# Block attention and a GELU MLP on one core: the first tile's order of products, and V of the second tile on two queues

## The chip, the core and the metric

The kernel runs on one core of a Trainium2 chip. A core has TensorE (matrix products into PSUM banks), VectorE, ScalarE and GpSimd, and SyncE (SP), which here only issues transfers. Each engine works through its own list in order and waits on semaphores. 16 DMA engines carry the transfers; SP and ScalarE can both issue them. The metric is the time of one execution on the device, in microseconds. Before the change it was 269.75 us, the median of three runs (269.55, 269.75 and 271.49).

## The reference

Two stages. The first is attention within chunks of 64 keys, for 8 batches, 8 heads, 576 positions and a head size of 64:

```python
q_c, k_c, v_c = (a.reshape(8, 8, 9, 64, 64) for a in (q, k, v))
scores = 0.125 * np.matmul(q_c, k_c.transpose(0, 1, 2, 4, 3))
attn = np.exp(scores - scores.max(-1, keepdims=True))
attn = attn / (attn.sum(-1, keepdims=True) + 1e-09)
out = np.matmul(attn, v_c)
```

The second takes those rows as x, 4608 tokens of 512, and computes `h = x @ w_in` (512 to 2048), `g = 0.5 * h * (1 + erf(h / sqrt(2)))`, and `g @ w_out` (2048 to 512). Inputs and output are float32.

## The kernel before

**Tiles.** The tokens go in 9 tiles of 512. Tile t below 8 holds the first 512 positions of batch t; the last tile holds the ninth chunk of all batches. Each tile passes three stages: attention, which leaves x transposed in SBUF (512 features as 4 slices of 128 partitions, 512 columns of tokens, one slice for each pair of heads); mm1, the product with w_in and the GELU, which leaves h in 16 blocks of 128 features; and mm2, the product with w_out, whose rows are stored. All products run in bfloat16.

**Order.** `tc.manual_schedule()` keeps every engine's instructions in the order in which the program's text issues them. While TensorE does mm1 and mm2 of one tile, the attention of the next one is put between the products, by hand: `phase` takes a table from a slot number to the steps that stand ahead of that slot. So a late operand of a step stops everything behind it on the same engine.

**The first tile** has no tile before it, so its attention stands alone (lines 965 to 1015). Per pair of heads g there are transposes of q and k (`T`), scores (`att_S`), and 1/sum: pairs 0 and 1 by `att_sum` on VectorE, pairs 2 and 3 by `att_sum_pe`, which forms the sums on TensorE, takes the reciprocal on VectorE (`i2`, `i3`) and spreads it over the partitions by 16 float32 products (`p2`, `p3`, line 484); ScalarE copies the result from PSUM (line 487). Then `att_av` multiplies by V (line 498, 64 by 64 products), 32 products for each two pairs, and `att_x` multiplies its result by the reciprocals on VectorE (line 506) and writes x. Where TensorE would stand idle, `keep_warm(n)` (line 958) issues n products of a tile of zeros, 512 columns each; there are 24.

**mm1 of the first tile** begins with `mm1_begin` (line 552): three blocks of h, each the sum of four products of 512 columns over the slices ks of x; first the slices 0 and 1 of all three blocks, then 2 and 3. Their PSUM banks come from the pool `ps_mm`, which has three. `mm1_slot` (line 538) then does block after block. w_in arrives in four chunks of four blocks and is cast to bfloat16 block by block on VectorE, GpSimd and ScalarE (line 939); w_out likewise in four chunks (line 947).

**mm2 of the first tile** (line 891) goes block by block of h over all rows, with the second tile's attention in between: transposes at the slots 2, 3, 4, 7, 8 and 9, scores (line 386) at 8 and 10, AV (line 418) at 13 and 14. ScalarE copies the transposed q and k of the first two pairs (line 178).

**Transfers.** SP issues all loads, in the order of the text. Loads go into five stage buffers of 1 MB, two more hold w chunks; a load waits until the casts from its buffer are done. V of the second tile (`load_v_plain`, line 149) is four transfers of 256 KB behind w_out's chunks; GpSimd casts them (`cast_v_plain`, line 156) behind its casts of w_out.

## Time and profile before

| | before |
|---|---|
| median of three runs | 269.75 us |
| the profiled execution | 270.41 us |
| its span | 268.6 us |
| TensorE busy in the span | 259.6 us, 97% |
| VectorE, ScalarE, GpSimd busy | 202.1, 187.1, 77.0 us |
| first product of mm1 | 18.56 us |
| first product of mm2 | 32.6 us |
| granted TensorE clock | 0.996 of full |

The span is the time from the first to the last instruction of the profiled execution; the rest of its time, 1.8 us, lies around it. All positions below are microseconds from the start of the span. A busy share says how long an engine had work in it, not that this work was needed: the products of zeros count as busy too. "The chain that ended last" follows the last instruction back, at each step to what released it or to the instruction ahead of it on its engine, and so shows what set the end. A row of the timeline merges instructions of one form that follow each other; the time in brackets is how long the engine was idle ahead of them, and what ended that.

### The profile page before, as it was taken

The page shows a single profiled execution, that of the slowest core. Times are in us where ns is not written, and L with a number is a line of the kernel's source. Part 1 is how long each engine was busy: PE and PEld are TensorE (multiplying, and loading weights), DVE is VectorE, ACT ScalarE, POOL GpSimd, SP SyncE. Part 2 cuts the span into 40 slices and gives each one's busy share as a digit, 9 for nine tenths or more (in the row PEclk, how much of TensorE's full clock was granted, in tenths as well). Part 3 has the DMA queues.
Part 4 walks back from the last instruction along what each step waited for, and adds up shares of the span by engine and source line. Part 5 has one row for each costly group of instructions (what it writes and reads, how often), then busy time and mean ns, then how long its engine had stood idle before and what let it go on. Part 6 is the DMA issues. An engine that isn't in the chain of part 4 may idle for free.

```text
span 268.6 us, 7554 instructions
## 1 busy us (share of the span) xinstructions
PE 259.6 (97%) x3077; PEld 195.6 (73%) x3092; DVE 202.1 (75%) x372; ACT 187.1 (70%) x364; POOL 77.0 (29%) x130
## 2 busy tenths in 40 slices
PE   7989999999999999999999999999999999999993
PEld 3554454476548654888888888888888888888882
DVE  2565775989997879589569956995699769958961
ACT  3466756797767967897689669957995799239700
POOL 3735667361440061441044103500362030000000
PEclk9999999999999999999999999999999999999998
DMA  7999999997979959999899989988886760430005
GB/s 230 285 377 402 395 388 243 237 286 194 336 205 261 244 123 231 279 237 191 232 232 231 177 216 242 264 152 206 237 193 146 166 192 0 89 138 12 2 2 156
DMA packets 127075, 56.59 MB, mean 211 GB/s; under 512 B 103488, under 2 KB 120896, under 8 KB 127040
## 3 DMA queue, kind: packets, MB, share of 16 engines
q1 hardware_dynamic: 126592, 55.59, 79.4%
q10 hardware_dynamic: 448, 0.52, 0.7%
q8 instruction: 24, 0.39, 0.6%
q14 instruction: 11, 0.09, 0.1%
HBM read 36.70 MB, written 9.44 MB: 172 GB/s over the span
## 4 chain that ended last, share of the span: by engine, by line
PE 92%; ACT 2%; DVE 1%; DMA 1%; issue 1%; POOL 0%; SPq 0%; ACTq 0%; DVEq 0%; POOLq 0%
PE y_ps L746 24%; PE h_Y L677 15%; PE y_ps L866 12%; PE h_Z L677 10%; PE h_X L677 10%; PE h_ps L538 6%; PE y_ps L891 4%; PE y_ps L755 4%; PE s_ps L247 2%; PE h_ps L699 1%; DMA arrival<-in_k_dram 1%; PE tp L170 1%; ACT y_ps L782 1%; PE warm L958 1%; PE rc_ps L484 1%
## 5 line engine op out<-in xcount | busy, mean ns | idle before, releaser
L677 PEld LDWEIGHTS <-w_in_s 128*128 128x128 bf16 x480 | 46.8, 98 | 6.1
L677 PEld LDWEIGHTS <-w_in_sb 128*128 128x128 bf16 x360 | 35.1, 98 | 6.5
L677 PE MATMUL h_X<-x,w_in_sb 128*128 128x256 bf16 x240 | 33.7, 272 | 0.0
L677 PE MATMUL h_Y<-x_t,w_in_s 128*128 128x256 bf16 x240 | 32.7, 272 | 0.0
L866 PE MATMUL y_ps<-w_out_sb,h 128*128 128x512 bf16 x137 | 31.7, 379 | 0.9 <-issue 0.8
L746 PEld LDWEIGHTS <-h_s 128*128 128x128 bf16 x304 | 29.7, 98 | 3.6 <-issue 0.2
L746 PEld LDWEIGHTS <-h 128*128 128x128 bf16 x288 | 27.8, 98 | 3.4
L218 POOL CAST v_nat<-arrival 128x1024 bf16<-128x1024 f32 x14 | 14.8, 1061 | 48.4 <-DMA arrival<-in_v_dram 48.3
L164 POOL CAST q_nat<-arrival 128x512 bf16<-128x512 f32 x33 | 19.4, 627 | 28.2 <-DMA arrival<-in_q_dram 19.1
L164 POOL CAST k_nat<-arrival 128x512 bf16<-128x512 f32 x34 | 21.9, 678 | 14.0 <-DMA arrival<-in_k_dram 10.1
L746 PE MATMUL y_ps<-w_t,h_s 128*128 128x256 bf16 x208 | 24.8, 273 | 0.0
L866 PEld LDWEIGHTS <-h 128*128 128x128 bf16 x144 | 13.3, 98 | 15.0 <-issue 0.2
L746 PE MATMUL y_ps<-w_out_sb,h 128*128 128x256 bf16 x192 | 22.9, 273 | 0.0
L963 ACT ACT_TABLE_LOAD x16 | 20.5, 1283 | 1.0 <-PEq L1199 0.7
L684 ACT ACTIVATE h<-h_Y 128x512 bf16<-128x512 f32 x30 | 17.7, 595 | 2.4 <-PE h_Y L677 1.9
L714 ACT COPY h_Y<-h_X 128x512 f32<-128x512 f32 x30 | 17.0, 582 | 2.8 <-PE h_X L677 2.6
L684 ACT ACTIVATE h<-h_X 128x512 bf16<-128x512 f32 x30 | 17.8, 597 | 1.4 <-PE h_X L677 0.6
L677 PE MATMUL h_Z<-x_t,w_in_s 128*128 128x256 bf16 x120 | 18.0, 273 | 0.0
L677 PE MATMUL h_Y<-x,w_in_s 128*128 128x256 bf16 x120 | 17.7, 273 | 0.0
L677 PE MATMUL h_Z<-x_t,w_in_sb 128*128 128x256 bf16 x120 | 17.4, 272 | 0.0
L725 DVE COPY h_a<-h_Y 128x512 f32<-128x512 f32 x8 | 5.5, 692 | 14.1 <-PE h_Y L677 14.1
L254 ACT ACTIVATE pT<-s_ps 128x512 bf16<-128x512 f32 x28 | 14.5, 601 | 2.3 <-PE s_ps L247 2.3
(148 smaller groups left out, 489.4 us busy)
## 6 DMA issues: line engine op xcount, KB each, us to landing
arrival<-in_q_dram SPq DMA_DIRECT2D x7, 1024.0 KB
arrival<-in_k_dram SPq DMA_DIRECT2D x24, 256.0 KB
out_dram<-y_sb SPq DMA_DIRECT2D x23, 256.0 KB
arrival<-in_v_dram SPq DMA_DIRECT2D x20, 256.0 KB
arrival<-in_moe_w_out_dram SPq DMA_DIRECT2D x4, 1024.0 KB
arrival<-in_v_dram SPq DMA_DIRECT2D x30, 128.0 KB
out_dram<-y_sb SPq DMA_DIRECT2D x5, 512.0 KB
arrival<-in_moe_w_in_dram SPq DMA_DIRECT2D x4, 512.0 KB
```

Source lines behind the costliest of these rows:

```text
L164: copy(st[nm][:, g].rearrange("p j r d -> p r j d"), st[nm + "f"][:, 2 * g:2 * g + 2])
L218: copy(st["v"][:, part[0], part[1], :D], st["vf"][:, part[0], part[1]])
L254: nc.scalar.activation(pT[:].rearrange("p u (c j) -> p u c j", j=J), s_ps[g2][c][:].rearrange("p u (j c) -> p u c j", j=J), Act.Exp, scale ...
L538: nc.tensor.matmul(h_ps[a][:], w_in_sb[:, ks, f * P:(f + 1) * P], st["x"][:, ks, :], start=(ks == 0), stop=(ks == KS - 1))
L677: nc.tensor.matmul(banks[g + name][:, i], lhs[:, kk, i], rhs[:, kk], start=fresh and i == kk == 0, stop=(kk == 1), skip_group_check=True)
L684: nc.scalar.activation(h[:, j:j + 2, m], src[:], Act.Gelu)
L714: AC(banks[g + "Y"][:], banks[g + "X"][:])
L746: nc.tensor.matmul(out[m], lhs[:, f, m * P:(m + 1) * P], rhs[:, f, :], start=fresh and f == 0 and (m == 0 or len(out) == 3), stop=(f == FH ...
L755: nc.tensor.matmul(out[m], lhs[:, f, m * P:(m + 1) * P], rhs[:, f, :], start=False, stop=(f == FH - 1), skip_group_check=True)
L866: nc.tensor.matmul(y_ps[:], st["h"][:, f, ms * P:(ms + 1) * P], w_out_sb[:, f, :], start=(f == 0), stop=(f == FF - 1))
L891: nc.tensor.matmul(tiles[t]["y_ps", ms][:], tiles[t]["h"][:, f, ms * P:(ms + 1) * P], w_out_sb[:, f, :], start=(f == 0), stop=False)
L963: nc.scalar.activation(act_scratch[:], rest[:, 0:1], func)
```

## The change

In the first tile:

- `att_av` of the pairs 0 and 1 is issued whole, ahead of the second spread `p3`, and `att_x` goes pair by pair: eight operations of 256 columns in place of four of 256 and two of 512.
- Two casts of w_in's first chunk (block 0 on GpSimd, block 1 on ScalarE) stand ahead of `p3`; block 3 goes from VectorE to GpSimd.
- `mm1_begin` takes a list of (block, slice). The products (0,0) and (1,0) come right behind `p3`, ahead of AV of the pairs 2 and 3. Behind that AV come the slices 0 and 1 of four blocks, then slices 2 and 3 of the blocks 0 and 1 and of 2 and 3. The fourth block's bank comes from `ps_at`, and each GELU is issued where its block is complete.
- `keep_warm` issues four products of 128 columns for each one of 512, and the tile of zeros is 128 columns wide.

In the second tile:

- Two of V's four transfers, and their casts, move to slot 5 of the first tile's mm2; ScalarE issues them, behind its copies of the slots 2 to 4.
- The casts of w_out's second chunk swap VectorE and GpSimd.

```diff
-    rest = consts.tile([P, 512], bf16, name="rest")
+    rest = consts.tile([P, P], bf16, name="rest")
...
-    def load_v_plain(t):
-        tiles[t]["vf"] = stage_tile()[:].rearrange("p (h n d) -> p h n d", h=H, d=D)
-        for n in range(CT // 2):
-            nc.sync.dma_start(tiles[t]["vf"][:, :, n], v[t, :, P * n:P * (n + 1), :].rearrange("h key d -> key h d"))
+    def load_v_plain(t, ns=range(CT // 2), engine=nc.sync):
+        if 0 in ns:
+            tiles[t]["vf"] = stage_tile()[:].rearrange("p (h n d) -> p h n d", h=H, d=D)
+        for n in ns:
+            engine.dma_start(tiles[t]["vf"][:, :, n], v[t, :, P * n:P * (n + 1), :].rearrange("h key d -> key h d"))
...
-    def att_x(t, g2, c, ns):
+    def att_x(t, g):
         st = tiles[t]
-        def part(p):
-            return p.rearrange("p g (n c e) -> p g n c e", c=2, e=CH)[:, :, ns[0]:ns[-1] + 1, c]
-        nc.vector.tensor_tensor(part(st["x"][:, 2 * g2:2 * g2 + 2]), st["av", g2][c][:, :, ns[0]:ns[-1] + 1],
-                                part(st["rcs", g2][:]), op=mybir.AluOpType.mult)
+        x, rc = (p.rearrange("p (n c e) -> p n c e", c=2, e=CH) for p in (st["x"][:, g], rc_of(t, g)))
+        for c in range(2):
+            nc.vector.tensor_tensor(x[:, :, c], st["av", g // 2][c][:, g % 2], rc[:, :, c], op=mybir.AluOpType.mult)
...
-    def mm1_begin(t, n):
+    def mm1_begin(t, order):
         st = tiles[t]
-        st["h"] = hpool.tile([P, FF, MT], bf16, tag="h", name="h")
-        h_ps = [ps_mm.tile([P, MT], f32, tag="mm", name="h_ps") for _ in range(n)]
-        order = [(f, ks) for k2 in range(2) for f in range(n) for ks in (2 * k2, 2 * k2 + 1)]
+        if "h" not in st:
+            st["h"] = hpool.tile([P, FF, MT], bf16, tag="h", name="h")
+            st["h_ps"] = {}
         for f, ks in order:
-            nc.tensor.matmul(h_ps[f][:], w_in_sb[:, ks, f * P:(f + 1) * P], st["x"][:, ks, :],
+            if ks == 0:
+                pool, tag = (ps_at, "at") if f == 3 else (ps_mm, "mm")
+                st["h_ps"][f] = pool.tile([P, MT], f32, tag=tag, name="h_ps")
+            nc.tensor.matmul(st["h_ps"][f][:], w_in_sb[:, ks, f * P:(f + 1) * P], st["x"][:, ks, :],
                              start=(ks == 0), stop=(ks == KS - 1))
-        for f in range(n):
-            nc.scalar.activation(st["h"][:, f, :], h_ps[f][:], Act.Gelu)
+            if ks == KS - 1:
+                nc.scalar.activation(st["h"][:, f, :], st["h_ps"][f][:], Act.Gelu)
...
-        for _ in range(n):
-            nc.tensor.matmul(warm[:], rest[:, 0:P], rest[:], start=True, stop=True)
+        for i in range(n * MT // P):
+            nc.tensor.matmul(warm[:, i % 4 * P:(i % 4 + 1) * P], rest[:], rest[:], start=True, stop=True)
...
-        att_av(0, 0, (0, 1))
-        for c in range(2):
-            att_x(0, 0, c, (0, 1))
+        att_av(0, 0)
+        att_x(0, 0)
+        att_x(0, 1)
+        win[0](0, PO)
+        win[0](1, AC)
         p3()
-        att_av(0, 0, (2, 3))
-        for c in range(2):
-            att_x(0, 0, c, (2, 3))
-        att_av(0, 1, range(4))
-        for c in range(2):
-            att_x(0, 1, c, range(4))
+        mm1_begin(0, [(0, 0), (1, 0)])
+        att_av(0, 1)
+        att_x(0, 2)
+        att_x(0, 3)
         win.append(load_w_in(NWC - 1))
         wout = [load_w_out(0)]
-        win[0](0, PO)
-        win[0](1, AC)
         act_table(Act.Gelu)
         win[0](2, PO)
-        win[0](3, DV)
-        mm1_begin(0, 3)
+        win[0](3, PO)
+        mm1_begin(0, [(0, 1), (1, 1), (2, 0), (2, 1), (3, 0), (3, 1)]
+                  + [(f, ks) for f2 in (0, 2) for ks in (2, 3) for f in (f2, f2 + 1)])
...
-        load_v_plain(1)
+        load_v_plain(1, (0, 1))
...
-            wout[1](i, DV if i % 2 == 0 else PO)
+            wout[1](i, DV if i % 2 == 1 else PO)
...
-        cast_v_plain(1, PO)
+        cast_v_plain(1, PO, (0, 1))
...
-                      2: [T[0]], 3: [T[2]], 4: [T[4], T[6]], 7: [T[1], T[3]], 8: [T[5], lambda: duo_S(1, 0)],
+                      2: [T[0]], 3: [T[2]], 4: [T[4], T[6]],
+                      5: [lambda: load_v_plain(1, (2, 3), nc.scalar), lambda: cast_v_plain(1, PO, (2, 3))], 7: [T[1], T[3]], 8: [T[5], lambda: duo_S(1, 0)],
...
-              by_rows=True, begun=3)
+              by_rows=True, begun=4)
```

9 lines of the change are left out of this document (4 added, 5 removed).

## The prediction

> **What bounds the kernel now.** I read the page first: TensorE's share, the engine shares of the chain that ended last, and TensorE's waits.
>
> ```profile
> span 268.6 us, 7554 instructions
> ...
> PE 259.6 (97%) x3077; PEld 195.6 (73%) x3092; DVE 202.1 (75%) x372; ACT 187.1 (70%) x364; POOL 77.0 (29%) x130
> ...
> PE 92%; ACT 2%; DVE 1%; DMA 1%; issue 1%; POOL 0%; SPq 0%; ACTq 0%; DVEq 0%; POOLq 0%
> ...
> PE av_ps L498 <- issue: 0.7, 1, 0.7
> ```
>
> TensorE carries 92% of the chain, so the time falls only where TensorE idles or works for nothing. Its longest single wait, after the one for its first operand, is in AV of the first tile (line 498), and it waits there for nothing that the profile shows. The change edits the first 47 us, so I read the chain there in order of time (start, us, what).
>
> ```profile
> 5.87 2.10 PE warm L958 x7
> 7.97 0.22 PE tp L170 x4
> 8.19 0.43 PE warm L958 x2
> ...
> 16.12 1.09 PE rc_ps L484 x16
> 17.22 0.44 PE av_ps L498 x39
> 17.66 0.70 issue
> 18.35 0.29 PE av_ps L498 x9
> ...
> 20.08 1.46 PE h_ps L552 x6
> 21.54 8.42 PE h_ps L538 x39
> ...
> 41.23 0.38 PE s_ps L386 x32
> 41.61 0.32 PE y_ps L891
> ...
> 47.49 0.38 PE av_ps L418 x32
> ```
>
> From 21.54 on the matmuls of 512 columns follow each other at 8.42/39 = 0.216 us and nothing waits: steady state. Before that, between the end of the second reciprocal spread (16.12 + 1.09 = 17.22) and 21.54, TensorE does 48 small AV products and 12 large ones, some 0.6 + 2.6 us of work in 4.3 us. That is where there is something to take.
>
> **The first tile, step by step.** The timeline has what each step needs (start, us, engine, line; idle before).
>
> ```profile
> 15.30 0.61 POOL L939 CAST w_in_sb<-arrival 128x512 bf16<-128x512 f32 x1 [0.73 <-DMA arrival<-in_moe_w_in_dram]
> ...
> 15.69 0.59 ACT L487 COPY rcs<-rc_ps 128x512 f32<-128x512 f32 x1 [0.48 <-PE rc_ps L484]
> ...
> 15.75 0.32 PE L498 MATMUL av_ps<-pT,v_nat 64*64 64x64 bf16 x16
> 15.86 0.21 DVE L477 RECIPROCAL rr<-sT 128x8 f32<-128x8 f32 x1 [0.51 <-PE sT L472]
> ...
> 16.13 0.76 DVE L506 TENSOR_TENSOR x<-av_ps,rcs 128x256 bf16<-128x256 f32 x2
> 16.62 0.61 POOL L939 CAST w_in_sb<-arrival 128x512 bf16<-128x512 f32 x1 [0.71 <-DMA arrival<-in_moe_w_in_dram]
> ...
> 17.27 0.59 ACT L487 COPY rcs<-rc_ps 128x512 f32<-128x512 f32 x1 [0.99 <-PE rc_ps L484]
> ...
> 17.75 0.62 ACT L939 CAST w_in_sb<-arrival 128x512 bf16<-128x512 f32 x1
> ...
> 18.56 2.97 PE L552 MATMUL h_ps<-x,w_in_sb 128*128 128x512 bf16 x11
> ```
>
> All 32 products of AV's first half now stand ahead of the spread. At 0.38/32 = 0.012 us each they end at 15.75 + 0.38 = 16.13; the spread waits for the reciprocal until 16.07 anyway, so it starts at 16.12 as before and ends at 17.22. Then:
>
> - x of head pair 0 is two VectorE operations of 256 columns, 16.13 + 0.76 = 16.89; pair 1 ends at 17.65. w_in's block 0 is cast at 15.91. Block 1 moves ahead of the second rcs copy on ScalarE: 16.28 + 0.62 = 16.90, and the copy behind it still starts at 17.27. Products (0,0) and (1,0) run 17.22 to 17.65.
> - AV's second half: 0.38, to 18.03, if the 0.70 does not come back. Its x follows on VectorE: pair 2 from 18.03 to 18.79, pair 3 to 19.55. Four operations of 256 cost 1.52 where two of 512 cost 1.30; the 0.22 stays under matmuls.
> - Six products on pairs 0 and 1, 6 x 0.216: 18.03 to 19.33. Block 2 is cast at 17.23, block 3, now on GpSimd behind it, at 17.84; the third bank of the pool is free when the rcs copy ends at 17.86. Pair 2 is needed at 19.33 (ready 18.79), pair 3 at 19.76 (ready 19.55, the tightest, 0.2 us to spare).
> - Eight more end at 21.05. All of four blocks are then done. Before, three were done at 21.54 and the fourth at 21.54 + 4 x 0.216 = 22.40.
>
> Gain **1.35 us**: 0.70 the gap, 0.2 AV moved into the wait for the reciprocal, 0.2 the wait for x (six products from 18.56 should end at 19.86; the next starts at 20.08), the rest the six that took 1.46 instead of 1.30.
>
> **The 0.70 gap** is the term without a price of its own, 0 to 0.70. What I see: the instruction queue q8 moves 24 packets in the whole execution (page), one of them between 16.0 and 17.2 us (DMA queues of that stretch); and TensorE has issued 222 + 223 instructions by the gap (stretches from the start).
>
> ```profile
> q8 instruction: 24, 0.39, 0.6%
> ...
> q8 instruction: 1, 0.02, 4.6%
> ...
> 8.78 0.32 PE L433 MATMUL s_ps<-qT,kT 64*64 64x64 bf16 x16
> ...
> 0.00:12.10 12.10, 10.16 (x96) 4.97 (x97) 4.75 (x10) 4.36 (x9) 6.29 (x21) 1.00 0.89 252
> 0.00:17.60 17.60, 15.46 (x222) 8.76 (x223) 8.30 (x19) 7.18 (x16) 8.70 (x24) 1.00 0.94 282
> ```
>
> A starved instruction stream fits: (3077 + 3092)/24 = 257 instructions a packet, so q8 feeds TensorE, and the gap comes where small products use instructions fastest. If a packet is asked for some 250 instructions ahead of its use, this one was asked for near instruction 193, at 12.1 us, and could be used at 18.35: 6.2 us. The 24 fillers of two instructions become 96, 144 instructions more. By the changed order, instruction 193 is then the end of the first scores (8.78 to 9.1 in this trace), and 445 is the start of AV's first half at 15.7. 9.1 + 6.2 = 15.3 is in time by 0.4 us. I take the gap as gone, nearer to this count than to "it stays"; the other end is 0.70. [...]
>
> **Fillers.** Their number is fixed, so columns count. Four transposes of 128 columns take 0.22 us and two fillers of 512 take 0.43, so a filler costs 0.22 instead of 0.215; nine on the chain lose 0.05 us. The shorter memset lets the first begin sooner, under the load of the first k, which ends later.
>
> **Carrying it on.** TensorE arriving 1.35 us earlier must find its inputs. The rows that set the tightest ones (a stretch with its DMA share and GB/s last, then the timeline):
>
> ```profile
> 31.00:42.00 11.00, 10.89 (x102) 5.93 (x102) 8.16 (x15) 6.82 (x12) 8.50 (x13) 1.00 1.03 352
> ...
> 25.55 1.62 POOL L939 CAST w_in_sb<-arrival 128x512 bf16<-128x512 f32 x2 [0.95 <-DMA arrival<-in_moe_w_in_dram]
> ...
> 31.41 10.61 SPq L149 DMA_DIRECT2D arrival<-in_v_dram  x4
> ...
> 33.40 1.55 POOL L947 CAST w_out_sb<-arrival 128x512 bf16<-128x512 f32 x2 [0.28 <-DMA arrival<-in_moe_w_out_dram]
> ...
> 36.92 1.07 ACT L178 COPY qT<-tp 128x512 bf16<-128x512 bf16 x2 [0.50 <-PE tp L170]
> ...
> 38.69 3.73 POOL L947 CAST w_out_sb<-arrival 128x512 bf16<-128x512 f32 x6 [0.97 <-DMA arrival<-in_moe_w_out_dram]
> ...
> 39.96 1.07 ACT L178 COPY kT<-tp 128x512 bf16<-128x512 bf16 x2 [1.96 <-PE tp L170]
> ...
> 45.70 0.63 POOL L156 CAST v_nat<-arrival 128x512 bf16<-128x512 f32 x1 [0.94 <-DMA arrival<-in_v_dram]
> ...
> 261.20 3.96 ACTq L847 DMA_DIRECT2D out_dram<-y_sb  x4
> ```
>
> The last w_in chunk is cast by 27.2; its first block is needed at 21.05 + 8 x 0.866 = 27.98. The second w_out chunk lands at 33.40, and the swap of VectorE and GpSimd has its first block cast at 34.2, needed near 35.8. The third is cast from 38.69, its first block by 39.31; it was needed at 41.61, now at 40.26: 0.95 to spare. V's last quarter is cast at 46.33; AV was at 47.49, now 46.14: 0.19 short if V stayed where it was.
>
> **V's second half** goes behind the qT copies on ScalarE's queue: 37.99 - 1.35 = 36.64. Queued behind it are the kT copies, which S waits for (41.03 to 41.23, 0.2 spare). ScalarE has 1.96 us free there, and the four issues at the kernel's end took at most 3.96/4 = 0.99 each, so two fit, just. SP's own four took 10.61/4 = 2.65 each in this stretch; that is the upper end, 5.3 us, and I take the lower because the row is ScalarE's own. For that the data passes the third and fourth w_out chunks: 0.52 MB at the 352 GB/s of this stretch moves them by up to 1.5 us. If the flow starts one issue later, at 37.6, the third chunk still had 1.1 us to run; at half rate that is 2.2, and its first block is cast at 40.41 against 40.26: **0.15 lost**, bounds 0 and 0.55 (38.69 + 1.5 + 0.62 = 40.8). V's casts follow the w_out casts: 38.69 + 3.73 + 4 x 0.65 = 45.0, at worst 46.5, 0.2 past AV's 46.14 + 0.15; I take none.
>
> SP, two issues shorter, goes on to q and k of the third tile sooner. GpSimd casts them after V, and nothing of them stands in the chain shown. If their bytes fill the engines while V's second half flows, that half shares with them instead of with w_out; its casts have 46.14 - 45.0 = 1.1 us for it.
>
> **Sum.** -1.35 + 0.05 + 0.15 = **-1.15 us**. The span becomes 267.45; the profiled execution, 270.41 for a span of 268.6, becomes 269.26. That execution lies 0.66 above the median of the three runs, 269.75, so the median becomes **268.6** (-0.4%). Nothing behind 50 us changes but its start.
>
> **Rivals.**
> - *The gap stays* (it belongs to AV's stream, or the earlier fetch is late all the same): -0.45, 269.3. For it: it sits in the second AV half, which still follows an uneven stretch. Against: the 144 instructions.
> - *ScalarE's queue blocks*, the slower side: each issue takes SP's 2.65 because the engines are full. The kT copies come 5.3 - 1.96 = 3.3 us late, S 3.1, and the 0.15 hides in it: 268.45 + 3.1 = 271.6. It decides from 1.1 us an issue; past 1% it needs some 3.1 us each. A single issue of 4.90 stands on SP's queue; two such would give 276. For it: the DMA share of 1.03 in that stretch. Against: SP's issues take long behind a backlog on SP's own queue; ScalarE's queue holds nothing before these two.
>
> ```profile
> 19.83 4.90 SPq L944 DMA_DIRECT2D arrival<-in_moe_w_out_dram  x1
> ```
>
> - *The change does not reach the chain*: the early products wait for x or bank and only reorder; the x of pair 3 late by 0.5. With 0.4 of the gain gone: 269.0. Against: the slacks above, of which only that 0.2 is thin.
>
> **How the numbers follow.** Forecast (268.1 to 268.9) 0.6; the gap stays or the reorder gives less 0.22; ScalarE blocks 0.12, a third of it past 1%; better than 268.0, 0.06. A measurement of this kernel tells about 1%, 2.7 us, from nothing. The sum never reaches that, so faster 0.03, same 0.92, slower 0.05. The range takes in the gap's return and the small end of blocking: 267.9 to 270.2. ScalarE blocking in full, 271.6 and up, lies above it, and the 0.06 below 268.0 is half outside.
>
> **What will show it.** Right: TensorE's wait list without line 498 or its like near 15.7; the fourth block's last product near 21.1; first w_out product near 31.4 instead of 32.76; S near 39.9. Wrong: a gap of 0.3 us or more before 22 us; DMA issues over 1 us on ScalarE near 37 us with S behind them; the third w_out chunk's cast after 40.3; a fetch gap at another dense stretch.

## The result and the profile after

The changed kernel takes **271.6 us** in the median (270.21 to 273.75), against 270.08 for the kernel before on the same chip (269.35 to 272.52). The ratio is 1.005, with a 95% interval of 1.0028 to 1.0073: by the ratio some 1.35 us slower, where 1.15 us faster was forecast, and outside the forecast range of 267.9 to 270.2. It is within 1%, as the chances said, but of the other sign, and the interval excludes no change.

The page of the changed kernel: its span, the busy time of TensorE, two DMA queues (packets, MB, share of the engines) and the chain's shares by engine.

```profile
span 270.1 us, 7702 instructions
...
PE 259.6 (96%) x3150; PEld 199.7 (74%) x3164; DVE 203.8 (75%) x373; ACT 187.2 (69%) x364; POOL 79.7 (30%) x131
...
q10 hardware_dynamic: 2528, 1.05, 1.5%
q8 instruction: 25, 0.41, 0.6%
...
PE 83%; DMA 7%; SPq 4%; issue 1%; POOL 1%; ACT 1%; DVE 0%; ACTq 0%; POOLq 0%
```

TensorE's busy time is what it was, 259.6 us. Its share of the chain fell from 92% to 83%, and DMA's rose from 1% to 7%: TensorE now waits for data. Its list of waits says where (total, times, longest).

```profile
PE av_ps L419 <- POOL v_nat L157: 0.7, 2, 0.3
...
PE h_ps L554 <- POOL w_in_sb L941: 0.3, 1, 0.3
PE h_Z L679 <- DVE h_d L730: 0.3, 1, 0.3
```

The wait of 0.70 in AV for "issue" is gone. Three others are new: for w_in's cast, for V's casts in the second tile, and for a VectorE operation on `h_d`, far behind the part that was edited. TensorE's timeline in the first tile shows the forecast order.

```profile
15.47 1.09 PE L485 MATMUL rc_ps<-ident_f,rr 128*64 128x128 f32 x16
16.84 0.60 PE L554 MATMUL h_ps<-x,w_in_sb 128*128 128x512 bf16 x2 [0.28 <-POOL w_in_sb L941]
17.37 0.45 PE L498 MATMUL av_ps<-pT,v_nat 64*64 64x64 bf16 x32
17.75 3.37 PE L554 MATMUL h_ps<-x,w_in_sb 128*128 128x512 bf16 x13
20.97 0.81 PE L537 MATMUL h_ps<-x,w_in_sb 128*128 128x512 bf16 x3
```

Four blocks are done at 21.13, forecast 21.05. The first w_out product starts at 31.33, 1.27 us ahead of the kernel before (32.60), forecast 1.35. That the places agree is luck. This execution had its first scores at 8.12 and its second spread at 15.47, where the kernel before, and with it the forecast, had 8.78 and 16.12. From the first scores to the first w_out product it is 23.21 us against 23.82: the reorder and the lost gap of 0.70 together brought 0.61; the other 0.66 of the lead is the earlier start. What the forecast had beyond that was waited away at w_in, as GpSimd's timeline shows:

```profile
16.17 0.61 POOL L941 CAST w_in_sb<-arrival 128x512 bf16<-128x512 f32 x1 [1.92 <-DMA arrival<-in_moe_w_in_dram]
17.57 1.17 POOL L941 CAST w_in_sb<-arrival 128x512 bf16<-128x512 f32 x2 [0.79 <-DMA arrival<-in_moe_w_in_dram]
```

Block 0 is cast at 16.78 and block 3 at 18.74, forecast 15.91 and 17.84. The lead of 1.27 stands until AV of the second tile begins at 46.15 (before: 47.42). It is spent as follows (start of the same step in both traces).

| step | before | after | lead |
|---|---|---|---|
| AV of the second tile, first half | 47.42 | 46.15 | 1.27 |
| AV of the second tile, second half | 48.76 | 48.67 | 0.10 |
| mm1 of the third tile | 54.51 | 54.24 | 0.27 |
| first w_out product behind the `h_d` wait | 120.78 | 120.87 | -0.09 |
| last product | 263.67 | 263.72 | -0.05 |
| end of span | 268.59 | 270.11 | -1.52 |

So there are three places: 1.17 us at V, 0.36 at `h_d`, 1.47 behind the last product. The chain in order of time shows the first (start, us, what).

```profile
32.06 11.94 DMA arrival<-in_v_dram
...
44.66 0.93 issue
...
45.61 1.76 POOL v_nat L157 x3
...
47.41 0.35 PE av_ps L419 x20
```

GpSimd's timeline of the same stretch, first of the kernel before, then of the changed one:

```profile
42.37 1.31 POOL L156 CAST v_nat<-arrival 128x512 bf16<-128x512 f32 x2
43.98 0.79 POOL L156 CAST v_nat<-arrival 128x512 bf16<-128x512 f32 x1 [0.30 <-DMA arrival<-in_v_dram]
```

```profile
44.05 0.61 POOL L157 CAST v_nat<-arrival 128x512 bf16<-128x512 f32 x1 [0.22 <-DMA arrival<-in_v_dram]
45.61 1.75 POOL L157 CAST v_nat<-arrival 128x512 bf16<-128x512 f32 x3 [0.95 <-DMA arrival<-in_v_dram]
```

Before, V's quarters land one behind the other (42.09, 43.00, 43.92 and 45.65 by the transfers' semaphores). Three are cast by 44.77, and one cast stands behind the last landing (it starts at 45.70, as the prediction's lines show): V is ready at 46.33. After, the second half is issued on ScalarE's queue at 36.01, but its first packet flows at 39.70, 0.39 us behind the first packet of the first half (39.31), and from there the two halves flow beside each other. Quarters 2, 0, 3 and 1 land in this order, at 43.51, 43.99, 45.29 and 45.55. The last landing is where it was before. But GpSimd casts in the order 0, 1, 2, 3, so it waits 0.95 us for quarter 1 while 2, and then 3, lie ready, and three casts stand in a row behind it: 47.36.

The second place, by VectorE's timeline of before and of after:

```profile
118.36 0.69 DVE L725 COPY h_d<-h_Y 128x512 f32<-128x512 f32 x1 [0.16 <-PE h_Y L677]
119.17 0.69 DVE L728 TENSOR_TENSOR h_d<-h_Z,h_d 128x512 f32<-128x512 f32 x1
```

```profile
118.09 0.69 DVE L727 COPY h_d<-h_Y 128x512 f32<-128x512 f32 x1 [0.16 <-PE h_Y L679]
119.25 0.69 DVE L730 TENSOR_TENSOR h_d<-h_Z,h_d 128x512 f32<-128x512 f32 x1 [0.47 <-PE h_Y L679]
```

From the copy's start to the addition's it is 0.80 before and 1.16 after. In the trace of after the semaphore wait ahead of the addition is over at 118.84, and the addition starts at 119.25: nothing that the profile names fills the 0.4 us.

The third place, by the DMA queues between 266.0 and 268.5 (packets, MB, share):

```profile
q10 hardware_dynamic: 173, 0.14, 17.3%
q1 hardware_dynamic: 105, 0.08, 10.9%
q8 instruction: 1, 0.02, 2.2%
```

TensorE's 25th instruction packet (16 KB) flows from 266.23 to 267.11, among the last stores. All store packets end by 266.92 except the last 20. These start at 267.10, where the instruction packet ends, and end between 267.24 and 268.19, strictly one behind the other. That they stood behind it on one DMA engine is argued from this order and not shown: the trace doesn't name the engine. Before, with 24 packets, the last store landed 3.1 us behind the last product; here it is 4.5.

### The profile page after: what moved, and what is told of

Read it like the earlier page. It is cut to its first block, busy times and chain, and to the rows that moved or that the text cites. A ratio compares the mean times of both kernels' runs of the same rounds, so it can differ in the third digit from the quotient of the medians.

```text
span 270.1 us, 7702 instructions
## 1 busy us (share of the span) xinstructions
PE 259.6 (96%) x3150; PEld 199.7 (74%) x3164; DVE 203.8 (75%) x373; ACT 187.2 (69%) x364; POOL 79.7 (30%) x131
## 4 chain that ended last, share of the span: by engine, by line
PE 83%; DMA 7%; SPq 4%; issue 1%; POOL 1%; ACT 1%; DVE 0%; ACTq 0%; POOLq 0%
PE y_ps L748 24%; PE h_Y L679 15%; PE y_ps L868 11%; PE h_Z L679 10%; PE h_X L679 10%; PE h_ps L537 5%; DMA arrival<-in_v_dram 4%; PE y_ps L757 4%; DMA arrival<-in_moe_w_in_dram 2%; SPq L150 2%; PE s_ps L248 2%; SPq L108 1%; PE h_ps L701 1%; ACT y_ps L784 1%; PE h_ps L554 1%
## 5 line engine op out<-in xcount | busy, mean ns | idle before, releaser
L219 POOL CAST v_nat<-arrival 128x1024 bf16<-128x1024 f32 x14 | 16.8, 1202 | 47.5 <-DMA arrival<-in_v_dram 47.4
```

Source lines behind the costliest of these rows:

```text
L219: copy(st["v"][:, part[0], part[1], :D], st["vf"][:, part[0], part[1]])
```

## The experiments

Theories at the start: **E**, the packet at the end makes the loss; **V**, moving V's half makes it; **I**, which came up later, the `h_d` wait belongs to VectorE's instruction count; **D**, the first 50 us go at the pace of the data, so that a lead is waited away. The expectations name further ones with their rivals. Ratios are to the kernel before on the same chip, with their 95% interval. An interval is some 0.5% wide (1.3 us), so a step of 0.4 us has to be read from a trace. The kernel before against itself gave 1.001.

| kernel | median us | ratio | first w_out product | V ready, AV starts |
|---|---|---|---|---|
| before | 270.08 | | 32.60 | 46.33, 47.42 |
| `before_again` | 270.83 | 1.0010 (0.9985 to 1.0035) | 32.03 | 47.04, 46.85 |
| after | 271.60 | 1.0050 (1.0028 to 1.0073) | 31.33 | 47.36, 46.15 |
| `after_again` | 271.32 | 1.0031 (1.0007 to 1.0055) | 32.91 | 49.86, 48.70 |
| `fewer` | 271.59 | 1.0052 (1.0026 to 1.0078) | 32.23 | 48.53, 47.08 |
| `more` | 271.88 | 1.0056 (1.0033 to 1.0079) | 32.06 | 48.83, 46.88 |
| `v_split_only` | 270.68 | 1.0020 (1.0005 to 1.0036) | 31.82 | 48.76, 47.02 |
| `fillers_only` | 270.95 | 1.0023 (1.0000 to 1.0046) | 32.04 | 47.55, 47.05 |
| `v_on_sp` | 270.78 | 1.0011 (0.9985 to 1.0036) | 32.18 | 47.90, 47.34 |
| `reorder_only` | 270.78 | 1.0009 (0.9990 to 1.0029) | 31.94 | 46.36, 46.75 |
| `chunk_out` | 270.60 | 1.0001 (0.9978 to 1.0024) | 31.70 | 45.32, 46.52 |
| `casts_swapped` | 270.92 | 1.0021 (0.9997 to 1.0045) | 32.61 | 48.02, 47.75 |
| `after_dve` | 270.87 | 1.0014 (0.9994 to 1.0035) | 32.91 | 48.43, 47.73 |
| `before_less_dve` | 270.59 | 1.0011 (0.9985 to 1.0038) | 32.62 | 46.93, 47.44 |
| `reorder_cast_dve` | 271.15 | 1.0027 (1.0001 to 1.0053) | 33.25 | 46.94, 48.07 |
| `reorder_dve` | 269.86 | 0.9978 (0.9955 to 1.0000) | 31.49 | 46.72, 46.31 |
| `v_on_sp_dve` | 270.76 | 0.9999 (0.9971 to 1.0027) | 31.89 | 47.64, 47.06 |
| `q2_behind` | 279.70 | 1.0342 (1.0310 to 1.0375) | 32.63 | 50.55, 48.73 |
| `reorder_spare` | 277.89 | 1.0288 (1.0246 to 1.0330) | 32.83 | 49.61, 48.33 |
| `v_on_sp_spare` | 278.77 | 1.0306 (1.0265 to 1.0347) | 31.90 | 50.12, 48.93 |

### The packet at the end

`fewer` takes instructions off TensorE, `more` adds some; the columns stay.

```diff
-    def keep_warm(n):
+    def keep_warm(n, cols=P):
         warm = ps_mm.tile([P, MT], f32, tag="mm", name="warm")
-        for i in range(n * MT // P):
-            nc.tensor.matmul(warm[:, i % 4 * P:(i % 4 + 1) * P], rest[:], rest[:], start=True, stop=True)
+        for i in range(n * MT // cols):
+            k = i * cols % MT
+            moving = rest[:, 0:cols] if cols <= P else rest[:, 0:1].to_broadcast([P, cols])
+            nc.tensor.matmul(warm[:, k:k + cols], rest[:, 0:P], moving, start=True, stop=True)
...
-        keep_warm(7)
+        keep_warm(7, MT)
         T = att_units(0, DV, AC)
```

> The changed kernel, with the first 28 fillers of 128 columns replaced by seven of 512: 42 instructions fewer on TensorE, the same columns. Theory E (a 25th instruction packet of 16 KB, fetched at 266.24 us, stands ahead of the last stores' packets on one DMA engine and lands them 1.4 us late): 24 packets, the last near 256, the last store packet ends some 1.4 us sooner against the last matmul, time 271.6 - 1.4 = 270.2. Rival N (the late landing is chance, or belongs to something else in the change): 271.6, and the end as late as in the changed kernel.

```diff
-        keep_warm(7)
+        keep_warm(7, 64)
         T = att_units(0, DV, AC)
```

> The changed kernel, with the first 28 fillers of 128 columns replaced by 56 of 64: 56 instructions more on TensorE, the same columns. Theory E: still 25 packets, but the last is asked for 56 instructions (28 products of 512 columns at 0.216 us, 6.0 us) sooner, near 260.2, when no store waits for its engine; the last store packet ends as in the kernel before, 270.2 in all. Rival M (each further packet costs, wherever it falls, or longer streams cost): 271.6 or more. Rival N (chance): 271.6.

The traces did what E says: 24 packets in `fewer`; in `more` the 25th at 260.49 (forecast 260.2); in both the last store lands 3.1 us behind the last product. The times did not follow: 271.59 and 271.88. So the late end belongs to that one execution. The same happened once more, in `v_on_sp_dve` (packet at 266.14, 4.5 us); with the same TensorE stream the packet came behind the stores in `v_on_sp` (270.70), and not at all in `after_again`.

> The changed kernel again, for a second profile. By what the variants showed: first w_out product between 31.3 and 32.2, V's last cast between 47.4 and 48.8, AV's wait 0.7 to 1.3, 0.3 for h_d near 119. The late end (theory E: a 25th instruction packet among the last stores, 1.4 us): if it is what makes the median, it is there again and the last store lands 4.5 us behind the last product; if it falls where it falls from execution to execution, 3.1 us.

There the last store lands 3.1 us behind the last product. The first product of w_out, at 32.91, and V, at 49.86, came later than I had expected. **E explains the 1.47 us in that trace and nothing of the median**, though the two agree to 0.1.

### V's half, and its casts

> The changed kernel, with the second half of V back on SP behind the first and its casts with the first half's: one part undone. Theory V (the half on ScalarE's queue makes three quarters of V land together, so that three casts stand in a row ahead of AV): V's last cast ends near 46.3 as in the kernel before, AV waits 0.2 instead of 1.2, and 1.0 us more of the lead is left at 50 us: 271.6 - 1.0 = 270.6, with the late end (theory E) still in it. Rival B (the bytes ahead of V are the same on either queue and the engines are full, so that V's last quarter lands at 45.6 whichever queue has it and AV waits the same): 271.4 to 271.6.

```diff
-        load_v_plain(1, (0, 1))
+        load_v_plain(1)
...
-        cast_v_plain(1, PO, (0, 1))
+        cast_v_plain(1, PO)
...
-                      5: [lambda: load_v_plain(1, (2, 3), nc.scalar), lambda: cast_v_plain(1, PO, (2, 3))], 7: [T[1], T[3]],
+                      7: [T[1], T[3]],
```

270.78 in place of 271.6, a ratio of 1.0011 in place of 1.0050, and AV waits 0.3 where the changed kernel, `after_again`, `fewer` and `more` wait 0.7 to 1.3. V counts. The 1.0 that should be left at 50 us is not there, though: this trace is 0.27 behind the kernel before at mm1 of the third tile, since it had waited 0.8 for w_in and 0.3 for w_out on the way. It loses another 0.55 at 74.96, by a wait for "issue" that comes up again under the first tile.

> The kernel before with the second half of V on ScalarE's queue and nothing else of the change. Theory V (the half moved makes V land late and in a lump): AV of the second tile waits 0.3 to 1.0 for V's casts, time 270.55 + 0.3 to 1.0 = 270.9 to 271.5. Rival (V on that queue is harmful only with the lead of the reorder in front of it): 270.5, AV's wait unchanged.

```diff
-        load_v_plain(1)
+        load_v_plain(1, (0, 1))
...
+                      5: [lambda: load_v_plain(1, (2, 3), nc.scalar), lambda: cast_v_plain(1, PO, (2, 3))],
```

Even without the reorder in front of it the half is harmful: AV waits 1.1, as theory V says. The time is less clear: 270.68 lies between what the theory and its rival forecast, and the ratio of 1.0020 is small, though its interval excludes 1. GpSimd's timeline and TensorE's waits of `v_split_only`:

```profile
45.44 0.62 POOL L157 CAST v_nat<-arrival 128x512 bf16<-128x512 f32 x1
47.00 1.76 POOL L157 CAST v_nat<-arrival 128x512 bf16<-128x512 f32 x3 [0.95 <-DMA arrival<-in_v_dram]
```

```profile
PE av_ps L419 <- POOL v_nat L157: 1.1, 3, 0.4
```

The same picture as in the changed kernel: one cast, 0.95 of waiting, three casts in a row. Two theories of it were tried against each other.

> The changed kernel with GpSimd's casts of the second tile's V in the order 0, 2, 3, 1 instead of 0, 1, 2, 3. In the changed kernel's profile the quarters 2 and 3 had landed on ScalarE's queue by 44.95 while GpSimd waited for quarter 1 until 45.61, and three casts then stood in a row to 47.36. Theory L (the lump: quarter 1 lands last, and two casts that could have gone before it go behind it): the last cast ends one cast behind the last landing, 1.1 us sooner against it; AV waits 0.1 to 0.3 instead of 0.7 to 1.3, 271.6 becomes 270.5. Rival Q (all four quarters land late, since q of the third tile flows beside them; the order matters little): 271.3 or more, AV's wait at least 0.6.

```diff
-        cast_v_plain(1, PO, (0, 1))
+        cast_v_plain(1, PO, (0,))
...
-                      5: [lambda: load_v_plain(1, (2, 3), nc.scalar), lambda: cast_v_plain(1, PO, (2, 3))], 7: [T[1], T[3]],
+                      5: [lambda: load_v_plain(1, (2, 3), nc.scalar), lambda: cast_v_plain(1, PO, (2, 3, 1))], 7: [T[1], T[3]],
```

```profile
45.71 2.31 POOL L157 CAST v_nat<-arrival 128x512 bf16<-128x512 f32 x4 [0.25 <-DMA arrival<-in_v_dram]
```

In GpSimd's timeline of `casts_swapped` the pause of 0.95 is gone, the four casts follow each other, V is ready 0.27 behind AV's start (1.21 in the changed kernel), and AV is not on TensorE's list of waits of 0.2 us or more. This trace runs later than the changed kernel's, so the two can't be compared by their times; but in it the quarters land at 45.66, 47.11, 44.93 and 46.73. In the old order the three casts behind quarter 1 would have ended near 47.11 + 1.8 = 48.9 (an estimate from the changed kernel, whose three casts end 1.8 behind that landing), 0.9 later than they did. 270.92, where L said 270.5; the interval of 0.9997 to 1.0045 touches that of the changed kernel, so the trace carries this more than the time does.

> The changed kernel with SP held, ahead of its loads of the third tile's q and k, until V's last cast (a copy of one row of it into a spare tile stands in front of them). Theory Q (with two issues less on SP, q of the third tile starts 3 us sooner and takes its share of the engines from V): V's last quarter lands 0.8 us or more sooner, AV waits 0.3 or less; 271.6 becomes 270.5, unless the third tile's own casts, 5 us later, are then waited for. Theory L: V lands as late as in the changed kernel, since the four quarters share the engines among themselves, and the three casts in a row stay: AV waits 0.7 or more, 271.3 or more.

```diff
+        hold = consts.tile([1, D], bf16, name="hold")
         def next_qk():
+            nc.sync.dma_start(hold[:], tiles[1]["v"][0:1, 0, 3, :D])
             for nm in "qk":
                 load_qk(2, nm)
```

With no byte of the third tile beside it V landed no sooner (48.8), and the row of three casts stayed. That speaks against Q, but weakly: this kernel ran with slower transfers for another reason (a 2 KB packet took 88.8 ns where the changed kernel's took 84.2; below), and its 279.7 says nothing on V. How much the third tile's q takes from V stays open.

> The changed kernel with the load of the fourth w_out chunk (1 MB) left out; its casts read the third chunk's arrival, so the output's second product is not the reference's. Theory D: V's bytes come 2.6 us sooner, AV of the second tile waits for no cast, 1.2 to 1.9 us are kept at 50 us and 271.6 becomes 269.7 to 270.4. Rival (V is late by its casts' order on GpSimd or by ScalarE's issue, not by the bytes ahead): the wait of 0.7 to 1.3 in AV stays, 271.2 or more.

```diff
-    def load_w_out(c):
-        raw = stage_tile(wsum if c > 1 else None)[:].rearrange("p (f n) -> p f n", f=FC)
-        nc.sync.dma_start(raw, w_out_v[:, c * FC:(c + 1) * FC, :])
+    def load_w_out(c, held={}):
+        if c == 2:
+            held["raw"] = stage_tile(wsum)[:].rearrange("p (f n) -> p f n", f=FC)
+        raw = held["raw"] if c > 1 else stage_tile()[:].rearrange("p (f n) -> p f n", f=FC)
+        if c != 3:
+            nc.sync.dma_start(raw, w_out_v[:, c * FC:(c + 1) * FC, :])
```

This kernel leaves out the load of one w_out chunk and serves for its time alone. With 1 MB less ahead of it V is ready at 45.32, AV waits for nothing, and 0.9 is kept to 120 us. 270.60, ratio 1.0001: by the ratio about 1.3 us off the changed kernel, as D said, but some 0.36 of it is the `h_d` wait, which this kernel does not have either. It then lost 1.3 us of its own at later places (0.27 near 140, 0.5 near 205, 0.55 near 220), which were not followed up.

### The first tile

> The kernel before, unchanged, for a second profile. The profiles of the changed kernel and of its four variants so far all had 5.2 to 5.6 MB moved by 20 us, that of the kernel before 5.9, and w_in, w_out and V follow that flow. Theory S (the early instruction packet at 10 us, which the 144 further instructions bring, takes its engine from the first loads): again 5.8 to 5.9 MB by 20 us and V's last cast near 46.3. Rival (the early flow varies by itself): anything from 5.2 to 5.9, and V's last cast up to 1.5 us later.

The early flow varies by itself: this trace moved 5.46 MB by 20 us and had V ready at 47.04, where the first trace of the same kernel had 5.93 and 46.33. Theory S is not excluded by that: seven traces with fillers of 512 columns moved 5.3 to 5.9 MB by 20 us, ten with smaller ones moved 5.1 to 5.7 (`fewer` and `more` among the ten, the three kernels with an added tile left out). The stretch from 0 to 20 us, last columns TensorE's clock, DMA share and GB/s, in the kernel before, in `before_again` and in `after_again`:

```profile
0.00:20.00 20.00, 17.12 (x236) 9.53 (x239) 10.23 (x23) 9.43 (x19) 9.31 (x25) 1.00 0.95 296
```

```profile
0.00:20.00 20.00, 17.65 (x239) 9.84 (x242) 10.81 (x24) 9.44 (x19) 9.04 (x25) 1.00 0.93 273
```

```profile
0.00:20.00 20.00, 18.08 (x314) 13.77 (x315) 10.09 (x24) 9.53 (x19) 9.26 (x25) 1.00 0.85 253
```

The trace that the prediction was made from had the fastest early flow of all. It also had a gap of 0.70 in AV that not every execution of this kernel has. TensorE's timeline of `before_again`:

```profile
16.01 1.09 PE L484 MATMUL rc_ps<-ident_f,rr 128*64 128x128 f32 x16
17.04 0.77 PE L498 MATMUL av_ps<-pT,v_nat 64*64 64x64 bf16 x48
18.22 2.75 PE L552 MATMUL h_ps<-x,w_in_sb 128*128 128x512 bf16 x11 [0.41 <-DVE x L506]
```

AV's 48 products run with hardly a break; TensorE then waits 0.41 for x, and the first w_out product stands at 32.03, 0.57 sooner than in the first trace. In the four traces with AV's order and the fillers of before, the instruction packet flows from 16.04 to 16.92 (gap 0.7), from 14.75 to 16.25 (`before_again`), from 13.90 to 15.32 (`v_split_only`, none) and from 16.18 to 17.14 (`before_less_dve` below, gap 0.9). Where TensorE stops it stops ahead of the same product, the 56th of AV's 64, and goes on 1.2 to 1.4 us behind the end of the packet: at 18.35, at 18.37, and in `before_again`, where only 0.18 us is lost, at 17.53. One more stop of this kind stands in `v_on_sp`, behind the AV of a later tile, 1.3 us behind a packet that ends at 73.66:

```profile
74.96 3.41 PE L868 MATMUL y_ps<-w_out_sb,h 128*128 128x512 bf16 x15 [0.55 <-issue]
```

So in these traces the gap goes with a late instruction packet, as the prediction took it; what was wrong is to take its size for a property of the kernel.

> The changed kernel with fillers of 512 columns again and V whole on SP: the reorder alone. Theory D (the first 50 us go at the pace at which w_in, w_out and V land, so that a lead on TensorE is mostly waited away): first tile up to 0.65 sooner (the gap of 0.70 is back somewhere, since the instruction count is that of the kernel before), at 50 us at most 0.4 ahead, and 270.1 to 270.7 against 270.55 for the kernel before. With S the early flow is that of the kernel before (5.8 to 5.9 MB by 20 us) and it is the fastest so far. Rival P (TensorE's own work sets the pace, the terms of the prediction hold): 0.65 kept to the end, 269.9 or less.

```diff
-    rest = consts.tile([P, P], bf16, name="rest")
+    rest = consts.tile([P, 512], bf16, name="rest")
...
-        for i in range(n * MT // P):
-            nc.tensor.matmul(warm[:, i % 4 * P:(i % 4 + 1) * P], rest[:], rest[:], start=True, stop=True)
+        for _ in range(n):
+            nc.tensor.matmul(warm[:], rest[:, 0:P], rest[:], start=True, stop=True)
```

(and V on SP, as above.) 270.78, ratio 1.0009. TensorE's waits of `reorder_only`:

```profile
PE h_ps L554 <- POOL w_in_sb L941: 0.8, 1, 0.8
...
PE h_Z L679 <- DVE h_d L730: 0.3, 1, 0.3
```

The early products stand where they should, and wait for w_in's blocks. At the first w_out product this trace is 0.66 ahead of the first trace of before, which has the gap, and 0.09 ahead of `before_again`, which hardly has it; 0.35 goes at `h_d`. The median of 270.78 is neither D's 270.1 to 270.7 nor P's 269.9, but nearer to D. From the first scores to the first w_out product it took 23.4 us in the traces with the old order and no gap (`before_again`, `v_split_only`, `fillers_only`). With the new order it took 22.7 to 24.7, on average of eleven traces 23.6 (`reorder_cast_dve` and the three kernels with an added tile left out). The 22.7 stand in `reorder_dve` and `after_dve`, the only two in which TensorE has no wait of 0.2 us or more for w_in. So the order by itself can save 0.7 us, and mostly doesn't, because the landing of w_in ends last: D is borne out in the first tile.

> The kernel before with the fillers of 128 columns and nothing else of the change: 144 instructions more on TensorE. Theory E: 25 packets, the last at the end of TensorE's stream in the middle of the last stores, which land 1.4 us late. Theory F (the gap of 0.70 in AV of the first tile is a fetch, whose place goes with the number of instructions): no gap in AV's second half. With both: start 0.2 to 0.66 sooner by the fillers, gap 0.70 gone, V at most 0.2 late, end 1.4 late: 270.1 - 0.9 to 1.3 + 1.4 = 270.2 to 270.6. Without E: 268.8 to 269.2. Without F: 0.7 more in either case.

```diff
-    rest = consts.tile([P, 512], bf16, name="rest")
+    rest = consts.tile([P, P], bf16, name="rest")
...
-        for _ in range(n):
-            nc.tensor.matmul(warm[:], rest[:, 0:P], rest[:], start=True, stop=True)
+        for i in range(n * MT // P):
+            nc.tensor.matmul(warm[:, i % 4 * P:(i % 4 + 1) * P], rest[:], rest[:], start=True, stop=True)
```

No gap, as F says; but 24 packets and not the 25 of E, and 270.95 is outside both forecasts (270.2 to 270.6, 268.8 to 269.2). With a ratio of 1.0023, its interval from 1.0000, and 1.0011 against 1.0009 for the reorder with and without them, the fillers' own effect is not settled; by the interval it is under 0.5%.

### VectorE's instruction count

> The reorder alone (fillers of 512, V on SP) with one more small memset on VectorE at the start, so that its instruction count is that of the kernel before. Theory I (the addition into h_d that starts 0.4 us behind its semaphore near 119 us is the place at which VectorE's instruction stream crosses a block; one instruction less ahead of it, the cast of w_in's block 3 that went to GpSimd, put the crossing there): TensorE's wait for h_d near 119 us is gone; 0.35 us better than the reorder alone, 270.4 against 270.78. Rival (the wait belongs to the arrival time of something else): the wait of 0.3 near 119 us stays.

```diff
     nc.vector.memset(rest[:], 0.0)
+    nc.vector.memset(rest[:, 0:2], 0.0)
```

**269.86**, ratio 0.9978. TensorE's waits of `reorder_dve` are, behind the first operand, these two, and the lead of 0.91 at mm1 of the third tile is 1.01 at the last product:

```profile
PE av_ps L420 <- POOL v_nat L158: 0.2, 1, 0.2
PE sum_ps L446 <- ACT pT L439: 0.2, 1, 0.2
```

> The kernel before with one instruction less on VectorE: the cast of w_in's block 3 in the first tile on GpSimd. Theory I (whatever instruction is number 192 of VectorE's stream starts some 0.4 us late; with one less it is the addition into h_d for which TensorE waits, with the full count it is the semaphore wait in front of it, where the time is hidden): a wait of 0.3 for h_d near 119 us appears in a kernel whose order is otherwise that of before, and the median goes up by 0.35 to 0.85 us, ratio 1.0013 to 1.003. Rival (the wait belongs to the reorder): no such wait, ratio 1.000.

```diff
         win[0](2, PO)
-        win[0](3, DV)
+        win[0](3, PO)
```

```profile
PE av_ps L498 <- issue: 0.9, 1, 0.9
PE h_Z L677 <- DVE h_d L728: 0.3, 1, 0.3
```

TensorE's waits of `before_less_dve`, above: the wait for `h_d` appears in a kernel that is otherwise the one before. The time between the starts of the `h_d` copy and the addition is 1.14 to 1.16 in every trace with one instruction less on VectorE (after, `after_again`, `fewer`, `more`, `v_on_sp`, `reorder_only`, `casts_swapped`, `q2_behind`, `before_less_dve`) and 0.79 to 0.80 in every one with the old count. `chunk_out`, with two less, also has 0.80. In the stream, number 192 is the addition with one less, behind a short semaphore wait. With the old count it is that semaphore wait, behind the copy of 0.69 us; with two less it is the next addition, behind one of 0.69 us. That the wait goes with VectorE's instruction count, and not with the reorder, is shown; what happens at number 192 is not. Its price is 0.36 us on TensorE (0.13%), which the ratio of 1.0011 with its interval neither shows nor denies.

> The changed kernel with one more small memset on VectorE at the start. Theory I: the wait for h_d near 119 us is gone; of the ratio 1.003 to 1.005 of the changed kernel 0.0013 to 0.003 goes, 1.001 to 1.003; what is left is V's casts (AV of the second tile waits 0.7 to 1.3). Rival (in the changed kernel everything is waited away at V, the later wait is shadowed): ratio unchanged, 1.004 or more.

The wait is gone, and 1.0014 is left of 1.003 to 1.005. AV waited 0.3 for V's casts there and not 0.7, because this execution had its first scores at 10.23, 2.1 us later than the changed kernel's 8.12; so the two effects are not cleanly apart in it.

> The reorder alone (fillers of 512, V on SP) with the cast of w_in's block 3 on VectorE as in the kernel before, so that the stream has its old count without a spare instruction. Theory I: no wait for h_d near 119 us, as with the spare memset, and a ratio of 0.996 to 0.999, below the reorder alone (1.0009). Rival (the gain of the spare memset was the execution's chance): the ratio of the reorder alone, 1.000 to 1.002.

```diff
-        win[0](3, PO)
+        win[0](3, DV)
```

No wait for `h_d`, but 1.0027: a miss. TensorE waits 1.0 us for this cast, which stands behind four x operations on VectorE. By this trace the cast is better placed on GpSimd, and the lost instruction has to be given back by something else.

### A spare tile

> The version that the runs point to: the reorder with block 3's cast on GpSimd, fillers of 512, V on SP, and the lost VectorE instruction given back as a spare memset of two columns behind that of ones_c, where no filler waits for it. If the first tile's reorder is worth what the spare memset showed: no wait for h_d near 119 us, first w_out product at 31.5 to 32.2, ratio 0.996 to 0.999. If that run was its execution's chance: 1.000 to 1.002.

> The same with fillers of 128 columns: the changed kernel without V's part, with VectorE's count restored. If the fillers are neutral (as 1.0011 with them against 1.0009 without, in the two kernels with the h_d wait): ratio 0.996 to 0.999, as the one beside it. Theory S' (the instruction packet that they bring to 10 us takes its engine from the first loads, 0.2 to 0.4 MB less by 20 us, V 0.5 to 1.0 us later): 0.5 to 1.0 us more than the one beside it, ratio 0.998 to 1.002.

```diff
     nc.vector.memset(ones_c[:], 0.0)
+    spare = consts.tile([P, 2], bf16, name="spare")
+    nc.vector.memset(spare[:], 0.0)
```

277.9 and 278.8. Neither expectation had this. The stretch from 22 to 40 us (last column GB/s), in `reorder_dve` and in `reorder_spare`:

```profile
22.00:40.00 18.00, 18.00 (x105) 8.99 (x103) 12.77 (x23) 12.07 (x21) 10.76 (x14) 1.00 1.06 398
```

```profile
22.00:40.00 18.00, 18.00 (x100) 8.77 (x99) 11.34 (x21) 12.33 (x22) 10.45 (x14) 1.00 1.06 373
```

The DMA engines are as busy (1.06 in both) and move 6% less (373 against 398 GB/s). By the addresses in the built programs, the tile of 4 bytes moves all later tiles by 32 bytes: the stage buffers start at 67,616 instead of 67,584.

> The changed kernel with V whole on SP and VectorE's count restored by a second memset into the fillers' own tile, so that no tile is added and no address moves. The two kernels with a spare tile of 4 bytes had all later tiles 32 bytes further on and took 277.9 and 278.8. If that shift of addresses is what they paid (their 2 KB packets took 88.6 ns on average against 84.2 to 84.5 elsewhere): 2 KB packets at 84 ns again, no wait for h_d near 119 us, ratio 0.997 to 1.000. If the memset or the count was what they paid: 1.02 or more.

Without the tile the 2 KB packets take 84.3 ns again and the ratio is 0.9999: it was the shift of addresses. It moves every tile behind the spare one; that the stage buffers are the ones that count is argued from their packets. Without the spare tile this kernel and `reorder_dve`, which differ in the fillers alone, stand at 0.9999 and 0.9978 with overlapping intervals. `reorder_dve` is the only kernel here clearly below the one before, and its interval ends at 1.0000: a gain of up to 0.4%, not a certain one, as among some twenty kernels one such interval can come about by chance.

## Why the prediction was wrong

- **What bounds the kernel** ("TensorE carries 92% of the chain, so the time falls only where TensorE idles or works for nothing"). True as a sum, wrong for the first 50 us. The trace before showed DMA shares near 1 in that stretch (0.95 from 0 to 20 us, 1.07 from 20 to 40), and I used them for single operands only. The data's landing varies between executions of one kernel (V of the second tile is ready at 47.36 in the changed kernel's first trace and at 49.86 in its second), so slacks of 0.2 us were no slacks.
- **First tile, 1.35 us.** This term was mis-sized, by 0.75 to 1.35 us. The 1.27 of the trace is luck: 0.66 of it is that this execution had its first scores sooner. 0.70 of the 1.35 was a gap that two of the four comparable traces of the old order do not have at that size, and the rest goes into waits for w_in, whose casts the prediction took at the times of the first trace. What the reorder is worth by itself is between nothing (`reorder_only`, 1.0009, with the `h_d` wait in it, and `v_on_sp_dve`, 0.9999) and 0.6 us (`reorder_dve`, 0.9978).
- **The gap as a late instruction packet.** The runs bear this link out: no trace with fillers of 128 columns has the gap in the first tile, and in the old order it comes and goes with the packet's time. The sign "a fetch gap at another dense stretch" came up once, in `v_on_sp`. The working was not right. That a packet is asked for some 250 instructions ahead of its use was the author's assumption; no trace shows when one is asked for. The packet's instructions were put in use from 9.1 + 6.2 = 15.3 us, 0.4 in time; the packet flowed from 10.12 to 10.99, and with the 1.2 to 1.4 us seen behind a packet's end they were there by some 12.4, an estimate from those traces. In the old order a packet that flows from 13.90 or 14.75 costs TensorE nothing or 0.18 us, one that flows from 16.04 costs 0.70 and one from 16.18 costs 0.9.
- **Fillers, 0.05.** Not resolved.
- **ScalarE's queue blocks**, the slower rival. It fell. The two issues took 0.43 and 0.59 us where at most 0.99 was allowed, and the kT copies were in time; scores began at 39.89, forecast 39.9, though by the head start and not as worked out. That the kernel came out at the rival's 271.6 is chance: it came there by another way. ScalarE's timeline:

```profile
36.01 0.43 ACTq L150 DMA_DIRECT2D arrival<-in_v_dram  x1
...
36.48 0.59 ACTq L150 DMA_DIRECT2D arrival<-in_v_dram  x1
```

- **Third w_out chunk, 0.15.** No loss at it in this trace (the lead stays 1.27), within the bounds, but not by the working: V's second half did not pass the w_out chunks from 37.6 on, its first packet flows at 39.70. In `after_again` TensorE waits 0.8 for w_out.
- **V's casts: "45.0, at worst 46.5, 0.2 past AV's 46.14 + 0.15; I take none."** This is the step that turned the gain into a loss. The sum counted only when GpSimd would be free, and took V's bytes as landed by then. I moved the issue of half of them and kept the casts' order. The halves flow beside each other, so the quarter that GpSimd takes second lands last (45.55), and what stands behind the last landing is three casts instead of one: ready at 47.36 and not 45.0. All nine traces with V's old place and no added tile have V ready between 1.1 us ahead of AV's start and 0.6 behind it. Six with the half moved, the casts in order and all loads in place have it behind: 1.2 to 1.95 (after, `after_again`, `fewer`, `more`, `v_split_only`) and 0.7 (`after_dve`). The clause that V would be "0.19 short if V stayed where it was" was not far off: 0.4 to 0.6 in `v_on_sp`, `v_on_sp_dve` and `reorder_dve`, though 0.4 ahead in `reorder_only`.
- **"Nothing behind 50 us changes but its start."** Failed: 0.36 us at 119 us, which goes with the cast of w_in's block 3 that moved to GpSimd. It had been counted as free because GpSimd had time for it; one instruction less on VectorE was what cost.
- **The sum.** With the measured terms: V's wait and the `h_d` wait (0.7 to 1.3, and 0.36) against a first tile worth 0 to 0.6 give 0.5 to 1.7 slower, where the sum had 1.15 faster; measured are 0.8 (`after_again`) and 1.35.

## What to carry to other kernels

Before a wait in one profile is booked as a gain, look at a second execution of the same kernel: here half of the forecast was a gap that half of the traces do not have, and later the end of one trace matched the whole loss and had nothing to do with it. A forecast position that comes out right is no proof either: count from the last point that the change did not touch. Here, with a DMA share of 1.16 from 38 to 46 us, splitting a load over two queues brought its parts in together (43.51, 43.99, 45.29 and 45.55, where they had landed at 42.09, 43.00, 43.92 and 45.65), and the operations behind the last landing were what counted: order the casts by landing, or leave the load in sequence. Moving or removing one instruction, or adding a tile of four bytes, changes every later place in that engine's stream and every later address. Here the one went with 0.36 us at number 192 of VectorE's stream and the other with some 8 us. So compare such details (count of instructions, addresses of the buffers) before blaming the edit itself.

## What the runs showed of the hardware

- **A fixed place in VectorE's stream.** In the nine traces in which number 192 of it is the addition behind a short semaphore wait, it starts some 0.36 us late (1.14 to 1.16 behind the copy's start against 0.79 to 0.80), and TensorE waits 0.3 for it. Where number 192 stands behind an operation of 0.69 us nothing shows; that it is late there too is argued, not shown. That the stream crosses a block there was theory I's reading of the count alone; no run shows it, and why at 192 stays open.
- **Addresses** (by the built programs). With the stage buffers at 67,584 (`reorder_dve`) the 2 KB packets from 22 to 40 us took 84.4 ns on average, and at 66,816 (the changed kernel, whose tile of zeros is 768 bytes smaller) 84.2. At 67,616 (`reorder_spare`) they took 88.7, and V's packets of 256 bytes some 21 ns against 18; at 66,944 (`q2_behind`) 88.8 and some 22.5. It is the written side of the loads, in SBUF, that moves. The two kernels with the spare tile took some 8 us of 270 more than the same kernels without it. What sets the two slow addresses apart, these runs don't tell.
- **An instruction packet among stores.** In the changed kernel's trace, behind a 16 KB packet of 0.88 us (266.23 to 267.11), 20 store packets came one by one until 268.19, while all others had ended by 266.92; the last store landed 4.5 us behind the last product instead of 3.1 (before).
- **The early flow.** From 253 (`after_again`) to 296 GB/s (before) in the first 20 us, by executions of kernels that issue the same loads; why, the runs don't tell.
